# All weights decoded in seven periods, two units at a place, and first expert blocks of 128 and 256 tokens

## The chip, the cores and the metric

The kernel runs on one NeuronCore of a Trainium2 chip. Its engines have queues of their own, each worked off in order: TensorE (PE, with its weight loads as PEld), VectorE (DVE), ScalarE (ACT), GpSimd (POOL), and SyncE (SP), which issues all transfers. The metric is the device time of one execution in microseconds (us), the median of several runs.

## The reference

Attention over 8 batches of 8 heads, 576 tokens and head dimension 64, in which each query keeps its 32 best scores; then a gated layer without activation over the 4608 rows of 512 values that the heads form.

```python
scores = scale * np.matmul(q, k.transpose(0, 1, 3, 2))
kth = np.partition(scores, -top_k, axis=-1)[..., -top_k:-top_k + 1]
scores = np.where(scores >= kth, scores, -1000000000.0)
attn = np.exp(scores - np.max(scores, axis=-1, keepdims=True))
attn = attn / (np.sum(attn, axis=-1, keepdims=True) + 1e-09)
x = np.matmul(attn, v)          # heads of a token side by side
...
a = x @ w1                      # 512 x 1024
b = x @ w2                      # 512 x 1024
h = a * b @ w3                  # 1024 x 1024
return h @ w_out                # 1024 x 512
```

All is float32. The kernel multiplies `w3` and `w_out` once, so that the layer has three products of weights: `w1`, `w2` and the folded `wf`.

## The kernel before, in words

**Slots and periods.** The attention is cut into 144 slots, 18 for each batch: a slot is one pair of heads and 128 queries (for the last 64 queries of a batch, two pairs of heads). The main loop runs over periods p = -1 to 146. In period p TensorE makes the scores of slot p + 1 (`st`), VectorE finds the 32 best of each row of slot p (`fold` into three parts, then MAX8 and MATCH_REPLACE8 by turns: the finder), ScalarE and GpSimd mask slot p - 1 and take its exponentials (`pab`), and TensorE transposes slot p - 2 (`tp`), multiplies it with the values (`ro`) and spreads its sums, after which VectorE normalises it (`rec`) and ScalarE and GpSimd split it into a high and a low part of the type fp32r (`x`).

**The experts.** Twelve slots give 384 tokens of all 512 values, a block. `moe_steps` is a generator of 288 matmuls for a block: for each of 8 parts of the 1024 hidden values twice 12 (`ab`, with weights `wh` and `wl`, the high and low parts), then for each of 4 parts of the output 24 (`eo`, with `wf`). The main loop calls `fill` three times a period, after the masks, after the first exponentials and after the values, and each call takes 8 of them: 24 a period, 288 in the twelve periods in which the next block is collected. The last block is worked off after the loop. Beside its matmuls a block needs, for each of the 8 parts, a copy and a rounding on ScalarE, a product on VectorE (`asb`) and a subtraction on GpSimd (`g`).

**Decoding the weights.** The weights come as 64-bit numbers whose float32 value has to be put together from their halves. There are 80 units of 128 x 256: 16 of `w_out`, then eight times 4 of `w3` and 2 of `w1`, then 16 of `w2`. A unit is a generator whose steps are taken one by one. Step 1: two activations on ScalarE, the first into half of a PSUM tile `t` (two units share a tile, lines 105 to 111), the second inside `z`, the tile that was fetched. Step 2: two operations on VectorE. Step 3: one addition on GpSimd. Step 4: nothing. Step 5: for `w1` and `w2` the high part on ScalarE, for `w3` two products with `wo` on TensorE (`pf`, 4 instructions in the trace). Step 6: the low part on GpSimd (`wl`), or, after each fourth unit of `w3`, the rounding of the folded product on ScalarE (`wf`); step 7: its rest on VectorE.

`warm` stands at six places of a period: after the fold, after the masks, after the first exponentials, after the finder's second round, after its third, and at the end. Before, from period 0 on, each of them starts one unit and takes one step of every unit under way, and then fetches, so that four tiles are on order. 80 units at 6 a period take periods 0 to 13. The first block is complete in period 13, and its matmuls begin in period 14.

**What sets the order.** Engines, wrapped in `InOrder`, get their instructions in the order in which the code is written; nothing sorts them. Transfers share SyncE's queue. Tiles `z` and the experts' `g` share eight buffers, `t`, `pf`, `ab` and `eo` share three PSUM tiles.

Of the kernel before, what the change touches and what calls it, by code (L numbers as in the profile page):

```python
# [19 lines left out]
NHP = H // 2  # L20
# [17 lines left out]
BLOCK = NS * NB // S  # L38
# [4 lines left out]
WAITING = 4  # L43
SHARE = 8, 8, 8
# [23 lines left out]
def attn_moe(ctx: ExitStack, tc: tile.TileContext, q, k, v, w1, w2, w3, w_out, out, flag, general):  # L68
# [354 lines left out]
    n_blocks = n_slots // BLOCK  # L423
    column, places = {}, []
    for n in range(n_blocks):
        mine = sorted({group_of[i] for i in range(n * BLOCK, (n + 1) * BLOCK)}, key=lambda g: groups[g])
        lo, pieces = 0, []
        for g in mine:
            b, t = groups[g]
            column[g], at_, w_ = lo, b * S + t * 128, width(t)  # L430
            if pieces and pieces[-1][0] + pieces[-1][2] == at_:
                pieces[-1][2] += w_
            else:
                pieces.append([at_, lo, w_])
            lo += w_
        assert lo == NB
        places.append([(lambda es, o=o, w_=w_: out[es, o : o + w_], slice(lo, lo + w_)) for o, lo, w_ in pieces])
# [9 lines left out]
    def fill(n):  # L447
        evict()
        while queue and n:
            if next(queue[0], "end") == "end":  # L450
                queue.pop(0)
            else:
                n -= 1

    def begin():
        while starting:
            n = starting.pop(0)
            queue.append(moe_steps([xs[n, hp] for hp in range(NHP)], NB, places[n], put_off.append))
# [22 lines left out]
    def warm():  # L481
        if p < 0:
            return
        if fetched:
            z, step = fetched.pop(0)
            going.append(step(z))
        going[:] = [unit for unit in going if next(unit, "end") != "end"]
        prefetch(WAITING)

    renew_q(0)  # L490
    for hp in range(NHP):
        kts[0, hp] = load_k(0, hp)
        if hp == 0:
            prefetch(WAITING)
    for hp in range(NHP):
        vts[0, hp] = load_v(0, hp)
    renew_q(1)
    for p in range(-1, n_slots + 3):
        i, j, m = p + 1, p - 1, p - 2
        finder = top32_steps(ss[p], p) if 0 <= p < n_slots else iter(())  # L500
# [14 lines left out]
        fill(SHARE[0])  # L515
# [8 lines left out]
        fill(SHARE[1])  # L524
# [21 lines left out]
        fill(SHARE[2])  # L546
        for _ in finder:
            pass
        if 0 <= m < n_slots:
            n = m // BLOCK  # L550
# [8 lines left out]
            if (m + 1) % BLOCK == 0:  # L559
                starting.append(n)  # L560
        warm()
    begin()
    while queue:
        fill(6)
# [63 lines left out]
```

## Time and profile before

| | |
|---|---|
| median of 3 runs | 1333.83 us (1333.48 to 1335.4) |
| the profiled execution's own time | 1335.09 us |
| its span | 1333.3 us |
| busy: PE, DVE | 1244.6 us (93%), 1194.2 us (90%) |
| busy: ACT, POOL | 977.0 us (73%), 750.6 us (56%) |
| mean granted TensorE clock | 0.977 |

Durations below come from the one profiled execution. Its span lies 1.8 us under its own time, and its own time 1.26 us over the median of the runs. Busy shares are means over the whole span: the first 210 us, in which weights are decoded, the steady state after 306 us and the last 63 us, in which one block is left, have different limits, so they are read apart.

### The profile page before, as it was taken

What the parts mean: (1) busy time and instruction counts of PE and PEld (TensorE: products, weight loads), DVE (VectorE), ACT (ScalarE), POOL (GpSimd) and SP (SyncE); (2) the same over time, 40 slices, a digit from 0 to 9 for tenths busy, and PEclk for the clock granted to TensorE, in tenths of its full rate; (3) what the DMA queues carried; (4) which work ended last, traced back from release to release, by engine and by line L of the source; (5) the groups of instructions that cost most, each with busy time, mean ns of one, the idle gap of its engine ahead of it and who ended that gap; (6) DMA issues with size and microseconds to landing.
All of it is one profiled execution on the core that took longest, in us unless ns stands there. A gap on an engine that the chain in (4) does not pass through costs nothing.

```text
span 1333.3 us, 29001 instructions
## 1 busy us (share of the span) xinstructions
PE 1244.6 (93%) x10001; PEld 1060.5 (80%) x10001; DVE 1194.2 (90%) x4012; ACT 977.0 (73%) x2185; POOL 750.6 (56%) x1097
## 2 busy tenths in 40 slices
PE   3677758999999999999999999999999999999996
PEld 1334436888888888888888888888888888888996
DVE  7988899999999999999999999999999999999610
ACT  5766777777777877778877777778777778778621
POOL 4666687655655655655645546645546556555510
PEclk9899978999999999999999999999999999999998
DMA  7233331200021001100120012100210012000000
GB/s 246 83 108 117 106 97 35 74 22 21 29 73 32 9 27 62 53 27 15 39 86 17 9 34 78 31 33 13 65 57 9 15 47 80 22 21 1 14 13 27
DMA packets 35890, 64.89 MB, mean 49 GB/s; under 512 B 6036, under 2 KB 12180, under 8 KB 35732
## 3 DMA queue, kind: packets, MB, share of 16 engines
q1 hardware_dynamic: 35732, 62.93, 14.7%
q8 instruction: 81, 1.33, 0.4%
q14 instruction: 77, 0.63, 0.2%
HBM read 53.48 MB, written 9.44 MB: 47 GB/s over the span
## 4 chain that ended last, share of the span: by engine, by line
PE 86%; DVE 6%; POOL 3%; issue 2%; ACT 2%; DMA 0%; POOLq 0%; SPq 0%
PE ab L57 32%; PE ro L57 16%; PE eo L57 16%; PE st L57 12%; PE tp L57 9%; DVE w L57 2%; DVE z L57 2%; PE pf L57 2%; POOL pab L57 1%; POOL z L57 1%; POOL wl L57 1%; ACT s L57 1%; DVE top L57 0%; ACT pab L57 0%; DVE wf L57 0%
## 5 line engine op out<-in xcount | busy, mean ns | idle before, releaser
L57 POOL TENSOR_TENSOR pab<-s,pab 128x576 f32<-128x576 f32 x288 | 403.7, 1423 | 218.3 <-PE ab L57 130.9
L57 DVE MAX8 top<-w 128x8 f32<-128x192 f32 (+1 forms) x1152 | 467.3, 447 | 0.0
L57 PE MATMUL ab<-x,wh 128*128 128x384 f32 x1536 | 402.6, 343 | 0.0
L57 DVE MATCH_REPLACE8 w<-top,w 128x192 f32<-128x192 f32 x864 | 289.4, 342 | 0.0
L57 ACT COPY pts<-tp 128x1024 f32<-128x1024 f32 x144 | 146.3, 1016 | 185.4 <-PE tp L57 185.4
L57 PEld LDWEIGHTS ab<-x,wh 128*128 128x128 f32 x1536 | 275.1, 189 | 0.0
L57 PE MATMUL ab<-x,wl 128*128 128x384 f32 x768 | 269.7, 351 | 0.0
L57 ACT ACTIVATE pab<-pab,edge 128x576 f32<-128x576 f32 x288 | 227.9, 791 | 0.7 <-POOL pab L57 0.7
L57 PE MATMUL eo<-g,wf 128*128 128x384 f32 x1152 | 225.6, 345 | 0.0
L57 PE MATMUL st<-kt,qt 64*128 64x288 f32 (+1 forms) x1280 | 188.7, 443 | 36.2 <-ACT pts L57 25.3
L57 ACT ACTIVATE pab<-s,edge 128x576 f32<-128x576 f32 x288 | 207.5, 768 | 4.1 <-POOL edge L57 3.9
L57 PEld LDWEIGHTS eo<-g,wf 128*128 128x128 f32 x1152 | 198.5, 188 | 7.5 <-issue 5.7
L57 ACT COPY s<-st 128x576 f32<-128x576 f32 x288 | 186.1, 647 | 17.7 <-PE st L57 17.7
L57 DVE TENSOR_TENSOR w<-s 128x384 f32<-128x384 f32 x288 | 186.7, 689 | 7.3 <-ACT s L57 7.3
L57 PEld LDWEIGHTS st<-kt,qt 64*128 64x128 f32 (+1 forms) x1280 | 100.6, 183 | 98.7 <-issue 41.6
L57 DVE TENSOR_TENSOR w<-w,s 128x384 f32<-128x384 f32 x288 | 165.8, 576 | 4.9
L57 PE MATMUL tp<-ident,pab 128*128 128x128 f32 x1152 | 151.3, 275 | 10.0 <-ACT s L57 9.9
L57 PE MATMUL ro<-pts,vt 128*64 128x128 f32 (+1 forms) x2560 | 157.2, 267 | 0.0
L57 PEld LDWEIGHTS ab<-x,wl 128*128 128x128 f32 x768 | 144.3, 188 | 13.6 <-issue 12.5
L57 PEld LDWEIGHTS tp<-ident,pab 128*128 128x128 f32 x1152 | 135.8, 142 | 21.2 <-POOL wo L57 10.7
L57 PEld LDWEIGHTS ro<-pts,vt 128*64 128x64 f32 x2560 | 137.8, 140 | 0.0
L57 POOL TENSOR_TENSOR g<-asb,g 128x384 fp32r<-128x384 f32 x96 | 97.0, 1010 | 69.6 <-ACT g L57 69.6
(49 smaller groups left out, 1246.7 us busy)
## 6 DMA issues: line engine op xcount, KB each, us to landing
z<-in_w SPq DMA_DIRECT2D x64, 256.0 KB, 2.7
vt<-in_v SPq DMA_DIRECT2D x32, 352.0 KB, 3.6
qt<-in_q SPq DMA_DIRECT2D x40, 256.0 KB, 2.7
kt<-in_k SPq DMA_DIRECT2D x32, 320.0 KB, 3.0
out_t<-osb SPq DMA_DIRECT2D x32, 192.0 KB, 1.9
z<-in_wo SPq DMA_DIRECT2D x16, 256.0 KB, 4.2
out_t<-osb SPq DMA_DIRECT2D x16, 160.0 KB, 1.8
out_t<-osb SPq DMA_DIRECT2D x16, 32.0 KB, 1.6
```

Source lines behind the costliest of these rows:

```text
L57: ins = fn(*args, **kw)
```

## The change

Three things change.

- `UNITS = 2`: each call of `warm` starts a unit and takes a step of all units, and does so twice. `warm` runs in period -1 too. So 12 units are started in a period, 80 in periods -1 to 5. Three tiles are on order instead of four.
- Keys and values of batch 0 are loaded one pair of heads at a time, keys in periods -1 to 2 and values in periods 0 to 3, where all were loaded ahead of the loop. The second tile of queries is loaded in period 0.
- `CUTS`: the first block is 4 slots (128 tokens), the second 8 (256 tokens), then eleven of 12 (384 tokens). A block's share for each call of `fill` follows from the periods in which the next block is collected: 12 matmuls for the first block (8 periods), 8 for all others. The first block's matmuls begin in period 6, the second's in period 14, the third's in period 26.

```diff
--- before.py
+++ after.py
@@ -35,13 +35,13 @@
 
 
 NS = len(slots_of(0))
-BLOCK = NS * NB // S
+CUTS = [0, 4] + list(range(NS * NB // S, B * NS + 1, NS * NB // S))
 NEG = -3.0e38
 STEEP = 2.0**80
 SCALE = 0.125
 S_BUFS = 3
-WAITING = 4
-SHARE = 8, 8, 8
+WAITING = 3
+UNITS = 2
 
 
 class InOrder:
@@ -420,10 +420,11 @@
         if not groups or groups[-1] != (b, t):
             groups.append((b, t))
         group_of.append(len(groups) - 1)
-    n_blocks = n_slots // BLOCK
-    column, places = {}, []
+    n_blocks = len(CUTS) - 1
+    block_of = [n for n in range(n_blocks) for _ in range(CUTS[n], CUTS[n + 1])]
+    column, places, widths = {}, [], []
     for n in range(n_blocks):
-        mine = sorted({group_of[i] for i in range(n * BLOCK, (n + 1) * BLOCK)}, key=lambda g: groups[g])
+        mine = sorted({group_of[i] for i in range(CUTS[n], CUTS[n + 1])}, key=lambda g: groups[g])
         lo, pieces = 0, []
         for g in mine:
             b, t = groups[g]
@@ -433,7 +434,7 @@
             else:
                 pieces.append([at_, lo, w_])
             lo += w_
-        assert lo == NB
+        widths.append(lo)
         places.append([(lambda es, o=o, w_=w_: out[es, o : o + w_], slice(lo, lo + w_)) for o, lo, w_ in pieces])
     last_use = {(b, hp): i for i, (b, hps, t) in enumerate(slots) for hp in hps}
 
@@ -444,10 +445,11 @@
         while put_off:
             put_off.pop(0)()
 
-    def fill(n):
+    def fill():
         evict()
+        n = queue[0][1] if queue else 0
         while queue and n:
-            if next(queue[0], "end") == "end":
+            if next(queue[0][0], "end") == "end":
                 queue.pop(0)
             else:
                 n -= 1
@@ -455,7 +457,9 @@
     def begin():
         while starting:
             n = starting.pop(0)
-            queue.append(moe_steps([xs[n, hp] for hp in range(NHP)], NB, places[n], put_off.append))
+            fills = 3 * (CUTS[n + 2] - CUTS[n + 1]) if n + 1 < n_blocks else 36
+            steps = moe_steps([xs[n, hp] for hp in range(NHP)], widths[n], places[n], put_off.append)
+            queue.append((steps, -(-3 * (2 * NCC * NFC + NFC * NEC) // fills)))
 
     def of(table, b):
         return {hp: table[b, hp] for hp in range(NHP) if (b, hp) in table}
@@ -479,24 +483,24 @@
             fetched.append((fetch(src), step))
 
     def warm():
-        if p < 0:
-            return
-        if fetched:
-            z, step = fetched.pop(0)
-            going.append(step(z))
-        going[:] = [unit for unit in going if next(unit, "end") != "end"]
-        prefetch(WAITING)
+        for _ in range(UNITS):
+            if fetched:
+                z, step = fetched.pop(0)
+                going.append(step(z))
+            going[:] = [unit for unit in going if next(unit, "end") != "end"]
+            prefetch(WAITING)
 
     renew_q(0)
-    for hp in range(NHP):
-        kts[0, hp] = load_k(0, hp)
-        if hp == 0:
-            prefetch(WAITING)
-    for hp in range(NHP):
-        vts[0, hp] = load_v(0, hp)
-    renew_q(1)
+    kts[0, 0] = load_k(0, 0)
+    prefetch(WAITING)
     for p in range(-1, n_slots + 3):
         i, j, m = p + 1, p - 1, p - 2
+        if i + 1 < NHP:
+            kts[0, i + 1] = load_k(0, i + 1)
+        if 0 <= p < NHP:
+            vts[0, p] = load_v(0, p)
+        if p == 0:
+            renew_q(1)
         finder = top32_steps(ss[p], p) if 0 <= p < n_slots else iter(())
         if 0 <= m < n_slots:
             invert(pabs[m][1])
@@ -512,7 +516,7 @@
             for a in range(2):
                 mask(ss[j], edges[j], pabs[j][0], a, folded if a == 0 else None)
         warm()
-        fill(SHARE[0])
+        fill()
         begin()
         next(finder, None)
         if 0 <= m < n_slots:
@@ -521,7 +525,7 @@
         if 0 <= j < n_slots:
             exps(edges[j], *pabs[j], 0)
         warm()
-        fill(SHARE[1])
+        fill()
         next(finder, None)
         warm()
         if i < n_slots:
@@ -543,11 +547,11 @@
             renew(vts, load_v, m)
         next(finder, None)
         warm()
-        fill(SHARE[2])
+        fill()
         for _ in finder:
             pass
         if 0 <= m < n_slots:
-            n = m // BLOCK
+            n = block_of[m]
             for hp in hps:
                 if (n, hp) not in xs:
                     xs[n, hp] = new_x()
@@ -556,12 +560,13 @@
             for part in fresh:
                 split_high(*part)
             del ss[m], pabs[m], edges[m]
-            if (m + 1) % BLOCK == 0:
+            if m + 1 == CUTS[n + 1]:
                 starting.append(n)
         warm()
     begin()
     while queue:
-        fill(6)
+        queue[0] = queue[0][0], 6
+        fill()
     evict()
 
     worst = small.tile([128, B + 1], F32, tag="worst", name="worst", bufs=1)
```

The scheduling of the places shows in each engine's queue. On ScalarE, around the copies of the scores in a period that decodes `w3` and `w1`; `t` and `z` are a unit's two activations, `s` the scores, `pab` the second exponential, `rec` the spread sums, `x` the high part of the normalised slot. Before:

```order
L57 ACTIVATE t_740<-z_660 128x256
L57 ACTIVATE z_660<-z_660 128x256
L57 ACTIVATE t_740<-z_674 128x256
L57 ACTIVATE z_674<-z_674 128x256
L57 COPY s_764<-st_758 128x2x288
L57 ACTIVATE pab_697,sums_698<-pab_697,edge_693 128x576
L57 COPY s_764<-st_761 128x2x288
L57 COPY rec_780<-ro_726 128x128
L57 ACTIVATE t_791<-z_691 128x256
L57 ACTIVATE z_691<-z_691 128x256
L57 CAST x_798<-rec_780 128x128
L57 ACTIVATE t_791<-z_711 128x256
```

The same stretch now:

```order
L57 ACTIVATE t_614<-z_594 128x256
L57 ACTIVATE z_594<-z_594 128x256
L57 COPY s_635<-st_629 128x2x288
L57 ACTIVATE pab_539,sums_540<-pab_539,edge_536 128x576
L57 COPY s_635<-st_632 128x2x288
L57 COPY rec_653<-ro_579 128x128
L57 ACTIVATE t_666<-z_603 128x256
L57 ACTIVATE z_603<-z_603 128x256
L57 ACTIVATE t_666<-z_617 128x256
L57 ACTIVATE z_617<-z_617 128x256
L57 CAST x_682<-rec_653 128x128
L57 ACTIVATE t_690<-z_627 128x256
```

Both units of a shared `t` (`t_666`) now stand together behind the copies; before, one of them (`t_791`) stood there, and the other behind the cast.

On VectorE, the end of the same period; `z` are a unit's two operations, MAX on `w` the last round of the finder, `rec` the normalising. Before:

```order
L57 TENSOR_SCALAR z_674<-t_740 128x256
L57 SCALAR_TENSOR_TENSOR z_674<-t_740,z_674 128x256
L57 MAX top2_97<-w_678 128x8 x2
L57 TENSOR_TENSOR rec_780<-ro_726,rec_780 128x128
L57 TENSOR_SCALAR z_691<-t_791 128x256
L57 SCALAR_TENSOR_TENSOR z_691<-t_791,z_691 128x256
L57 RECIPROCAL sums_698<-sums_698 128x2
```

Now:

```order
L57 TENSOR_SCALAR z_594<-t_614 128x256
L57 SCALAR_TENSOR_TENSOR z_594<-t_614,z_594 128x256
L57 TENSOR_SCALAR z_603<-t_666 128x256
L57 SCALAR_TENSOR_TENSOR z_603<-t_666,z_603 128x256
L57 MAX top2_97<-w_511 128x8 x2
L57 TENSOR_TENSOR rec_653<-ro_579,rec_653 128x128
L57 TENSOR_SCALAR z_617<-t_666 128x256
L57 SCALAR_TENSOR_TENSOR z_617<-t_666,z_617 128x256
L57 TENSOR_SCALAR z_627<-t_690 128x256
L57 SCALAR_TENSOR_TENSOR z_627<-t_690,z_627 128x256
L57 RECIPROCAL sums_540<-sums_540 128x2
```

The first unit that ScalarE starts behind its copies (`z_603`) is decoded ahead of the finder's last round; before, the unit that stands there (`z_691`) was decoded behind it and behind the normalising.

On TensorE, after the last product of decoded weights; `st` are scores, `tp` and `ro` belong to a finished slot. Before, no block is ready yet:

```order
L57 MATMUL tp<-ident,pab 128x128 x8
L57 MATMUL ro<-ident,pab 128x128
L57 MATMUL st<-kt,qt 128x288 x4
L57 MATMUL ro<-ident,sums 64x128 x2
L57 MATMUL ro<-pts,vt 64x128 x8
L57 MATMUL ro<-pr,vt 64x128 x2
```

Now the first block's matmuls of 128 tokens stand between, twelve at a place, three times a period (the last four of one place, then the next):

```order
L57 MATMUL ab<-x,wl_103 128x128
L57 MATMUL ab<-x,wh_98 128x128 x2
L57 MATMUL ab<-x,wl_103 128x128
L57 MATMUL tp<-ident,pab 128x128 x8
L57 MATMUL ro<-ident,pab 128x128
L57 MATMUL ab<-x,wh_99 128x128 x2
L57 MATMUL ab<-x,wl_983 128x128
L57 MATMUL ab<-x,wh_99 128x128 x2
L57 MATMUL ab<-x,wl_983 128x128
```

The transposes, the scores and the values, which stood next to each other, are parted by them.

## Rows read from the trace of the kernel before

**Rows 1.** Busy time of each engine by stretches: start and end of the stretch, its length, then busy us and number of instructions of PE, PEld, DVE, ACT and POOL, the granted TensorE clock, the share of the DMA engines and GB/s. The stretches end at the folds of periods 0, 14 and 26.

```profile
0.00:7.33 7.33, 2.29 (x8) 1.27 (x8) 0.00 (x1) 2.60 (x4) 1.03 (x9) 1.00 0.74 257
7.33:209.61 202.28, 132.76 (x650) 72.89 (x651) 178.27 (x529) 142.33 (x354) 136.30 (x188) 0.88 0.36 115
209.61:306.28 96.67, 94.47 (x884) 82.62 (x883) 93.37 (x321) 75.21 (x166) 59.20 (x87) 0.98 0.15 47
306.28:1258.08 951.80, 951.80 (x8073) 841.61 (x8072) 916.54 (x3150) 741.25 (x1628) 544.24 (x803) 1.00 0.11 35
```

**Rows 2.** Timeline of ScalarE in the steady state, the copies of two transposed slots: start, length, engine, line, operation, tiles, shape, and in brackets the idle time before it with what ended it.

```profile
1202.53 1.02 ACT L57 COPY pts<-tp 128x1024 f32<-128x1024 f32 x1 [1.30 <-PE tp L57]
...
1210.57 1.02 ACT L57 COPY pts<-tp 128x1024 f32<-128x1024 f32 x1 [1.31 <-PE tp L57]
```

**Rows 3.** The chain that ended last, its last two long pieces: start, length, what.

```profile
1270.39 33.92 PE ab L57 x192
1304.31 16.96 PE eo L57 x96
```

**Rows 4.** Timeline of VectorE in periods that decode `w3` and `w1`, folds and what ends its waits, and the fold of period 14.

```profile
89.08 1.54 DVE L57 TENSOR_TENSOR w<-s 128x384 f32<-128x384 f32 x2
...
105.50 1.54 DVE L57 TENSOR_TENSOR w<-s 128x384 f32<-128x384 f32 x2
...
108.32 0.41 DVE L57 TENSOR_SCALAR z<-t 128x256 int32<-128x256 int32 x1
...
109.10 0.68 DVE L57 TENSOR_TENSOR wf<-pf,wf 128x512 fp32r<-128x512 f32 x1
...
110.49 0.61 DVE L57 MAX8 top<-w 128x8 f32<-128x192 f32 x2
...
116.64 1.41 DVE L57 MAX8 top<-w 128x8 f32<-128x576 f32 x2
118.74 0.29 DVE L57 TENSOR_TENSOR rec<-ro,rec 128x128 f32<-128x128 f32 x1 [0.68 <-ACT rec L57]
119.39 0.42 DVE L57 TENSOR_SCALAR z<-t 128x256 int32<-128x256 int32 x1 [0.36 <-ACT z L57]
...
209.61 1.58 DVE L57 TENSOR_TENSOR w<-s 128x384 f32<-128x384 f32 x2
```

**Rows 5.** Timeline of GpSimd in the same period: the two masks together, and the addition of a unit.

```profile
109.57 2.78 POOL L57 TENSOR_TENSOR pab<-s,pab 128x576 f32<-128x576 f32 x2 [1.59 <-ACT pab L57]
...
113.00 0.72 POOL L57 TENSOR_TENSOR z<-z 128x256 int32<-128x256 int32 x1
```

**Rows 6.** Timeline of TensorE: products of decoded weights (four instructions are one unit) in three periods, and the eight transposes of a slot in the steady state.

```profile
103.55 3.70 PE L57 MATMUL pf<-wo,z 128*128 128x512 f32 x8
...
113.78 1.98 PE L57 MATMUL pf<-wo,z 128*128 128x512 f32 x4 [2.53 <-POOL z L57]
...
128.54 3.20 PE L57 MATMUL pf<-wo,z 128*128 128x512 f32 x4 [2.54 <-POOL z L57]
...
161.36 1.98 PE L57 MATMUL pf<-wo,z 128*128 128x512 f32 x4 [2.54 <-POOL z L57]
...
1209.44 1.03 PE L57 MATMUL tp<-ident,pab 128*128 128x128 f32 x8
```

**Rows 7.** Timeline of ScalarE in one decoding period, from the masks on.

```profile
108.73 1.43 ACT L57 ACTIVATE pab<-s,edge 128x576 f32<-128x576 f32 x2
...
111.28 0.99 ACT L57 COPY pts<-tp 128x1024 f32<-128x1024 f32 x1
...
116.49 0.64 ACT L57 COPY s<-st 128x576 f32<-128x576 f32 x1 [0.93 <-PE st L57]
117.03 0.78 ACT L57 ACTIVATE pab<-pab,edge 128x576 f32<-128x576 f32 x1
...
117.80 0.63 ACT L57 COPY s<-st 128x576 f32<-128x576 f32 x1
118.44 0.27 ACT L57 COPY rec<-ro 128x128 f32<-128x128 f32 x1
118.60 0.41 ACT L57 ACTIVATE t<-z 128x256 f32<-128x256 f32 x1
...
120.31 0.41 ACT L57 ACTIVATE t<-z 128x256 f32<-128x256 f32 x1 [0.76 <-DVE z L57]
```

**Rows 8.** The same view as in rows 1, of the whole period that begins with the fold at 105.50 and of two of the bursts in rows 6.

```profile
105.50:120.27 14.77, 11.18 (x59) 5.81 (x58) 13.32 (x42) 10.99 (x27) 10.17 (x14) 1.00 0.35 108
128.54:131.67 3.13, 3.13 (x4) 0.88 (x4) 2.96 (x11) 0.83 (x3) 2.69 (x4) 0.60 0.67 226
161.36:163.27 1.91, 1.91 (x4) 0.68 (x4) 1.78 (x8) 0.82 (x3) 1.91 (x3) 1.00 0.61 145
```

**Rows 9.** Timeline of ScalarE at the very start: its first copy of scores, and the second of two units that share a tile.

```profile
5.70 0.64 ACT L57 COPY s<-st 128x576 f32<-128x576 f32 x1 [3.69 <-PE st L57]
...
10.24 0.40 ACT L57 ACTIVATE t<-z 128x256 f32<-128x256 f32 x1 [2.29 <-DVE z L57]
```

**Rows 10.** Groups of instructions by form: line, engine, operation, tiles, shapes, number, then busy us and mean ns of one, then idle us before.

```profile
L57 PE MATMUL tp<-ident,pab 128*128 128x128 f32 x1152 | 151.3, 275 | 10.0 <-ACT s L57 9.9
...
L57 DVE TENSOR_TENSOR asb<-ab,asb 128x384 f32<-128x384 f32 x96 | 52.6, 548 | 32.5 <-PE ab L57 32.5
...
L57 DVE TENSOR_TENSOR rec<-ro,rec 128x128 f32<-128x128 f32 x144 | 42.0, 291 | 56.6 <-ACT rec L57 50.6
```

## The prediction, before the changed kernel was run

> **What bounds the kernel now.** I read the stages first [rows 1]. From 306.28 to 1258.08 us TensorE is busy all the time and VectorE 916.54 of 951.80 us. That is the steady state: one period takes 8.04 us, from one copy of the transposed weights to the next [rows 2], and VectorE works 7.74 us of it (96.3%). The last block runs alone at the end: 192 and 96 matmuls of 384 columns in 33.92 and 16.96 us, 0.177 us each [rows 3]. Neither stretch changes: the last eleven blocks have the same 384 tokens and the same turns. So the change is decided before 306.28 us: in the 14 periods in which weights are decoded (7.33 to 209.61 us) and in the 12 periods of the first block (96.67 us). In the 202.28 us of decoding VectorE is busy 178.27. All that VectorE does there has to be done in the changed kernel too; what a rearrangement can win is the 24 us that it waits, plus what the first 7.33 us leave idle, and it can lose any amount.
>
> Next I asked what VectorE waits for in one decoding period, 105.50 to 120.26 us. It is a ring through all engines. VectorE folds the scores, decodes a unit, splits a folded weight and decodes another until 110.49 [rows 4]; GpSimd masks for 2.78 us from 109.57 and only then adds the unit of which TensorE's product is next in line, at 113.00 [rows 5]; that product starts at 113.78 [rows 6]; behind it in TensorE's queue stand the scores, behind these ScalarE's two copies, an exponential and the copy of the sums at 118.44 [rows 7]. For these VectorE waits 0.68 us at 118.74, and for the next decode, queued behind them on ScalarE, 0.36 us more [rows 4]. Where TensorE runs at its lower level the same four instructions take 3.20 instead of 1.98 us [rows 6], with a mean granted clock of 0.60 against 1.00 [rows 8], and the period is 16.4 instead of 14.77 us: the folds at 89.08 and 105.50 lie that far apart [rows 4].
>
> **The change, part by part.** *Two units at a place.* Both units of a place share one PSUM tile, and ScalarE's activations of the second wait until VectorE has finished the first: before, 2.29 us at 10.24 and 0.76 us at 120.31 [rows 9, 7]. With one unit at a place the two engines are a whole place apart, and the finder's rounds lie between. With two, VectorE decodes the first unit in the same place in which ScalarE starts it, so at every place the order is ScalarE first unit, VectorE first unit, ScalarE second unit, and whatever ScalarE had to do earlier in the period now stands in front of VectorE.
>
> I lay one such period out by hand, with a unit at 0.75 us on ScalarE and 0.8 on VectorE (119.39 to 120.19) [rows 7, 4], counted from the fold. VectorE: fold 2.8, unit left over 0.8, weight split 0.6, first unit 0.8: 5.0. ScalarE: second unit 0.75, two masks 1.4, first unit of place 2 0.75: 7.9. VectorE decodes it: 8.7. ScalarE: second unit 0.75, pts and pr 1.1, exponential 0.8, first unit of place 3 0.75: 12.1. VectorE: 12.9. ScalarE: second unit; then the rounding of the fold product, which waits for TensorE. GpSimd can mask only from 6.5 (ScalarE's half of the masking stands behind its second unit), ends at 9.3, subtracts one low part and adds the first unit by 10.8 (0.7 each) [rows 5]; TensorE then needs about 1.7 us for each of two units, as pf x8 takes 3.70 with its tail [rows 6], and is done at 14.3. ScalarE: rounding 0.55, high part 0.35, first unit of place 4 0.75: 16.1; VectorE: 16.9. ScalarE: second unit 0.75, copy, exponential, copy, sums (2.1 together, from 116.49 to 118.60), first unit of place 5 0.75: 20.6. VectorE: unit 0.8, MAX8 over 576 1.35, normalising 0.3: 23.0. ScalarE: x 0.3, first unit of place 6 0.75: 24.1; VectorE 0.8: **25.0 us** with the passing of semaphores. VectorE's own work in it is 18.7 us: 13.32 in the period read above [rows 8], six more units of 0.8 and one more split of 0.6. So 6.3 us of waiting in one period that takes the place of two, which waited 1.5 and 3.1 us (14.77 and 16.4, less 13.32).
>
> The low level of TensorE's clock comes on top. The products now stand in groups of four units behind the values, then idle for 2 us and more until GpSimd has added again, then two units in front of the transposes and two in front of the scores. In this trace a burst after 2.54 us of idling ran once at the full and once at the lower level [rows 6, 8]. Nothing lost is one bound; the other is two units at half the clock, 3.4 us more. I take 1.2 us, the difference of the two rows: 26.2 us a period.
> The Trainium skill (TensorE: Matmul & The Clock Gate, "HAM oscillation — how this bites in real kernels") says that bursts parted by idle gaps each start at the lower clock, again and again. By that rule the last rival below would be the likeliest; the two bursts above agree with it one time in two.
>
> *The sum for decoding.* Period -1 now decodes 12 units with nothing between them: each pair costs ScalarE two units and VectorE one, 2.4 us, six pairs 14.4 us from about 5 us on (ScalarE's first work stood at 5.70 [rows 9]), and the copies of the first scores: the first fold near 20 us instead of 7.33. Period 0 has no masks and no values and is bound by VectorE: 18.7 less 0.5 for the sums and their product, 18.2. Period 1 has masks but no values: 24 (the ring without pts, pr and x, 1.4 us, and most of the clock's price). Periods 2 and 3: 26.2 each. Period 4: 26.4, with two more high parts of w2 in the ring. Period 5 has eight units of w2, which cost GpSimd two operations each, but no products: 21. Sum 162 us at the fold of period 6.
>
> *Eight periods with 128-token matmuls.* Each has 36 matmuls of 128 columns instead of none. The trace has no such matmul. Lower bound: in proportion to the columns, 0.059 us. Upper bound: a whole 384-column one, 0.177, or twice a transpose, 0.216. The nearest row is the transpose, which has the same 128 x 128 weight and 128 columns: eight in 1.03 us with a tail of 0.275, 0.108 each [rows 6, 10]. I take that: TensorE 36 x 0.108 + 3.8 = 7.7 us (3.8 is 8.04 less 24 x 0.177). VectorE: 7.74 less 0.37 (two thirds of an asb product of 0.548) plus 1.5 products of about 0.29, a PSUM product of 128 columns [rows 10]: 7.8. With the 0.3 us that the steady state adds: 8.1 us, eight periods 64.8. At the lower bound VectorE still makes it 8.1; at the two upper ones TensorE makes it 10.2 and 11.6.
> So the fold of period 14 comes at 226.8 us, where it came at 209.61 [rows 4]: **17.2 us later**. The seven periods are dear because attention is no cheaper alone than the steady 8 us.
>
> *The 256-token block.* 24 matmuls a period of at most 0.177 us: never dearer than before. If they are cheaper VectorE is the limit: 7.74 less 0.37 plus two thirds of 0.42 is 7.65 us, with some waiting 7.85, against 96.67 / 12 = 8.06 now. Twelve periods: 2.5 us won (0 to 4).
>
> *The rest.* Three tiles fetched ahead instead of four, eight buffers as before: a unit's transfer is issued when the unit five before it is done, over a place ahead of its use, some 4 us in these long periods. Keys and values come a period at a time, each one period or more before its use. I cost both at nothing; if a transfer does come late, ScalarE stands still and the period grows by as much.
>
> The sum: 17.2 - 2.5 = 14.7 us on the profiled execution's 1335.09, 1349.8; the median of the runs is 1.26 lower, so **1348.5 us**.
>
> **The rivals.** *Faster: the engines slip past each other.* If ScalarE runs ahead (its own work is 17 us of such a period: 10.99 [rows 8], six units, two high parts and a rounding more), the hand-laid ring is too strict, and periods 1 to 4 take 20 us each (VectorE's 18.7 and 1.3 of waiting) instead of 102.8 together: 23 us less, and period 5 4 us less: 1321.5. It decides once a decoding period is under about 22.5 us. For it: in the trace VectorE waits only 1.5 us in a good period. Against it: that is with one unit a place, and the queues are in order, so ScalarE cannot start a unit before the copies in front of it. *No change:* decoding periods of 22.5 us, 14 us less: 1334.5. *Much slower: narrow matmuls are not cheaper.* At 0.177 the eight periods take 10.2 us each, 17 us more: 1365.5; at 0.216 28 us more: 1376.5. For it: no row shows a matmul of this kind under 384 columns. Against it: transposes of 128 columns run at 0.108, and TensorE has 0.3 us a period to spare there.
> *Slower by the clock:* every group of products starts at the lower level, 2.2 us more in each of periods 1 to 4: 1357.5.
>
> **How the numbers follow.** The forecast gets 0.48, with a range of its own from 1339 to 1358 (5 us for the clock that stays up, and 4 to 9 us for the stretches that were only estimated); the clock that is always low 0.08, since it rose within a burst in this trace; the faster rival 0.18, no change 0.08, the narrow matmuls 0.18. A measurement of this kernel can tell 0.2%, 2.7 us. Slower by more than that: forecast, clock and narrow matmuls, 0.74; faster 0.18; within 0.08. The range runs from 1327, a third of the way out of the faster rival, to 1368, past the first price of the narrow matmuls.
>
> **What would show it.** Right: folds of periods 2 and 3 that lie 24 to 28 us apart, with VectorE idle 5 us and more before decodes that wait for ScalarE; the first 128-column matmul near 165 us; pitch near 0.11 us; the fold of period 14 near 227 us; the same 8.04 us after it; the same last 51 us. Wrong: decoding periods near 20 us (then faster), periods above 10 us with narrow matmuls (then slower still), or ScalarE waiting for transfers of z, which I cost at nothing.

## The result and the profile after

The changed kernel takes 1344.73 us (median of 4 runs, 1343.74 to 1346.71) against 1334.62 for the kernel before beside it: ratio 1.0074, 95% interval 1.0054 to 1.0095. It is slower, by more than the 0.2% that can be told, as forecast; 1348.5 was 3.8 us too high. The profiled execution took 1343.74 us with a span of 1341.9, the one before 1333.3.

The stages first, in the view of [rows 1]: start and end, length, then busy us and instructions of PE, PEld, DVE, ACT and POOL, granted clock, DMA share, GB/s. The stretches end at the folds of periods 0, 6, 14 and 26.

```profile
0.00:20.05 20.05, 4.58 (x16) 2.46 (x16) 8.89 (x23) 10.04 (x25) 8.15 (x19) 1.00 0.86 287
20.05:164.86 144.81, 89.48 (x319) 44.28 (x319) 108.39 (x300) 89.64 (x236) 90.55 (x131) 0.84 0.44 130
164.86:227.57 62.71, 60.30 (x582) 53.41 (x583) 60.65 (x218) 48.88 (x114) 41.95 (x59) 0.95 0.05 12
227.57:317.21 89.64, 84.42 (x933) 72.74 (x932) 89.15 (x323) 73.54 (x168) 64.09 (x84) 1.00 0.16 50
317.21:1266.70 949.49, 948.67 (x8048) 837.81 (x8048) 915.56 (x3150) 740.53 (x1627) 552.20 (x805) 1.00 0.12 35
```

The decoding periods fill the first two lines: VectorE works 108.39 of 144.81 us, where it worked 178.27 of 202.28 us. In the third and fourth line it is busy 97% and 99% of the time. Period 26 begins 317.21 - 306.28 = 10.9 us later than before; of the rest, 1341.9 - 317.21 = 1024.7 us, it took 1027.0 before.

The folds that begin periods 1 to 6, in VectorE's timeline (start, length, what):

```profile
38.51 1.57 DVE L57 TENSOR_TENSOR w<-s 128x384 f32<-128x384 f32 x2
63.54 1.57 DVE L57 TENSOR_TENSOR w<-s 128x384 f32<-128x384 f32 x2
89.32 1.57 DVE L57 TENSOR_TENSOR w<-s 128x384 f32<-128x384 f32 x2
115.86 1.58 DVE L57 TENSOR_TENSOR w<-s 128x384 f32<-128x384 f32 x2
141.97 2.10 DVE L57 TENSOR_TENSOR w<-s 128x384 f32<-128x384 f32 x2
164.86 1.57 DVE L57 TENSOR_TENSOR w<-s 128x384 f32<-128x384 f32 x2
```

Where a period goes is seen in period 2. ScalarE's timeline in it (in brackets the idle time before an instruction, and what ended it):

```profile
68.92 0.40 ACT L57 ACTIVATE t<-z 128x256 f32<-128x256 f32 x1 [3.46 <-DVE z L57]
...
69.58 1.43 ACT L57 ACTIVATE pab<-s,edge 128x576 f32<-128x576 f32 x2
70.91 0.38 ACT L57 ACTIVATE t<-z 128x256 f32<-128x256 f32 x1
71.23 0.41 ACT L57 ACTIVATE z<-z 128x256 int32<-128x256 uint16 x1
72.59 0.41 ACT L57 ACTIVATE t<-z 128x256 f32<-128x256 f32 x1 [0.95 <-DVE z L57]
72.95 0.42 ACT L57 ACTIVATE z<-z 128x256 int32<-128x256 uint16 x1
74.31 1.01 ACT L57 COPY pts<-tp 128x1024 f32<-128x1024 f32 x1 [0.95 <-PE tp L57]
```

And VectorE's in the same place 2:

```profile
71.68 0.42 DVE L57 TENSOR_SCALAR z<-t 128x256 int32<-128x256 int32 x1 [1.09 <-ACT z L57]
72.14 0.42 DVE L57 SCALAR_TENSOR_TENSOR z<-t,z 128x256 int32<-128x256 int32 x1
```

The first unit is activated at 70.91, decoded on VectorE at 71.68, and ended by 72.56; only then, at 72.59, does ScalarE start the second, after 0.95 us of idling. VectorE had waited 1.09 us for ScalarE just before. The engines take turns, pair by pair. VectorE's waits for ScalarE in period 2 sum up to (engine, what it waited for: us in total, times, longest):

```profile
DVE z L57 <- ACT z L57: 6.2, 5, 2.5
```

And over the second stage, in the same view:

```profile
ACT t L57 <- DVE z L57: 46.8, 35, 3.6
DVE z L57 <- ACT z L57: 28.7, 25, 3.2
```

The groups of TensorE's products in periods 2 and 3:

```profile
67.60 5.80 PE L57 MATMUL pf<-wo,z 128*128 128x512 f32 x8 [6.12 <-issue]
74.62 3.70 PE L57 MATMUL pf<-wo,z 128*128 128x512 f32 x8 [0.24 <-POOL z L57]
80.88 7.13 PE L57 MATMUL pf<-wo,z 128*128 128x512 f32 x16
93.38 6.56 PE L57 MATMUL pf<-wo,z 128*128 128x512 f32 x8 [5.37 <-issue]
```

The group behind the long idle time is slow and the later ones are not; the windows of the first two (columns as above) give the clock:

```profile
67.60:73.40 5.80, 5.80 (x10) 2.50 (x11) 3.79 (x13) 3.50 (x8) 3.99 (x6) 0.63 0.18 49
74.62:78.32 3.70, 3.70 (x10) 1.51 (x10) 1.29 (x4) 2.69 (x8) 2.21 (x4) 1.00 0.67 179
```

The first block's matmuls of 128 columns, in TensorE's timeline:

```profile
172.65 0.39 PE L57 MATMUL ab<-x,wh 128*128 128x128 f32 x2
172.87 0.27 PE L57 MATMUL ab<-x,wl 128*128 128x128 f32 x1
172.99 0.39 PE L57 MATMUL ab<-x,wh 128*128 128x128 f32 x2
```

Three start in 0.34 us (172.65 to 172.99): 0.113 each. Over the whole trace the median from one start to the next is 0.112 us at 128 columns, 0.119 at 256 and 0.176 at 384: the matmuls of the second block, with twice the columns, cost hardly more than those of the first. The steady state and the last block are what they were in [rows 2, 3], from ScalarE's timeline and the chain of waits:

```profile
1203.75 1.02 ACT L57 COPY pts<-tp 128x1024 f32<-128x1024 f32 x1 [1.31 <-PE tp L57]
1211.79 1.02 ACT L57 COPY pts<-tp 128x1024 f32<-128x1024 f32 x1 [1.31 <-PE tp L57]
```

```profile
1279.64 33.92 PE ab L57 x192
1313.56 16.96 PE eo L57 x96
```

### The profile page after: what moved, and what is told of

The parts are those of the page before. It is cut to its first block, busy times and chain, and to the rows that moved or that the text cites. A ratio compares the mean times of both kernels' runs of the same rounds, so it can differ in the third digit from the quotient of the medians.

```text
span 1341.9 us, 29628 instructions
## 1 busy us (share of the span) xinstructions
PE 1251.4 (93%) x10289; PEld 1073.4 (80%) x10289; DVE 1188.7 (89%) x4020; ACT 978.7 (73%) x2205; POOL 767.4 (57%) x1105
## 4 chain that ended last, share of the span: by engine, by line
PE 83%; DVE 8%; ACT 3%; issue 3%; POOL 2%; DMA 0%; SPq 0%; DVEq 0%; POOLq 0%; ACTq 0%
PE ab L57 31%; PE ro L57 15%; PE eo L57 15%; PE st L57 11%; PE tp L57 9%; DVE w L57 3%; DVE top L57 2%; DVE z L57 2%; PE pf L57 2%; POOL wl L57 1%; ACT z L57 1%; ACT pab L57 1%; POOL z L57 1%; ACT t L57 1%; ACT s L57 0%
## 5 line engine op out<-in xcount | busy, mean ns | idle before, releaser
L57 PE MATMUL ab<-x,wh 128*128 128x384 f32 (+2 forms) x1664 | 418.4, 335 | 2.7 <-POOL x L57 2.7
L57 PEld LDWEIGHTS ab<-x,wh 128*128 128x128 f32 x1664 | 292.4, 189 | 4.7 <-POOL x L57 2.9
L57 PE MATMUL ab<-x,wl 128*128 128x384 f32 (+2 forms) x832 | 282.9, 340 | 0.0
L57 ACT ACTIVATE pab<-pab,edge 128x576 f32<-128x576 f32 x288 | 227.5, 790 | 10.3 <-POOL pab L57 10.3
L57 PE MATMUL eo<-g,wf 128*128 128x384 f32 (+2 forms) x1248 | 232.1, 336 | 0.0
L57 PE MATMUL st<-kt,qt 64*128 64x288 f32 (+1 forms) x1280 | 184.8, 435 | 30.9 <-ACT pts L57 17.4
L57 PEld LDWEIGHTS eo<-g,wf 128*128 128x128 f32 x1248 | 205.1, 188 | 8.1 <-issue 6.3
L57 DVE TENSOR_TENSOR w<-s 128x384 f32<-128x384 f32 x288 | 178.8, 661 | 0.0
L57 PEld LDWEIGHTS ab<-x,wl 128*128 128x128 f32 x832 | 156.9, 189 | 12.5 <-issue 11.6
L57 PEld LDWEIGHTS st<-kt,qt 64*128 64x128 f32 (+1 forms) x1280 | 97.3, 178 | 85.7 <-issue 32.1
L57 POOL TENSOR_TENSOR g<-asb,g 128x384 fp32r<-128x384 f32 (+2 forms) x104 | 98.5, 947 | 69.6 <-ACT g L57 69.4
```

The source lines that it names most:

```text
L57: ins = fn(*args, **kw)
```

## The experiments

The theory at the outset: the loss lies in the decoding stage, because the two units of a place share a tile `t` and so tie ScalarE to VectorE; the narrow blocks give a part back. The rivals: narrow matmuls that are not cheaper, the clock, and the queue order of TensorE. The kernel before was run again beside each set of experiments, with medians from 1334.62 to 1336.34 us, so a difference between kernels of two sets is uncertain by up to 1.7 us; ratios are to the kernel before of the same set.

**The early decoding without the narrow blocks.**

```diff
-CUTS = [0, 4] + list(range(NS * NB // S, B * NS + 1, NS * NB // S))
+CUTS = list(range(0, B * NS + 1, NS * NB // S))
```

> The changed kernel with blocks of 384 tokens from the first on; decoding in seven periods stays. Theory (the decoding periods cost the time, the narrow blocks give some back): the fold of period 6 stays at 165 us; periods 6 to 13 have no expert matmuls and take VectorE's own 7.35 us, fold of period 14 at 224; the first block's twelve periods take 94 us, fold of period 26 at 318; the rest 1027 us. Time some 3 us above the changed kernel's, 11 to 13 above the kernel before. Rival (the narrow matmuls, with a weight load for every 128 or 256 columns, cost the time): with them gone the time falls to the kernel before's, within 3 us.

Measured: 1352.27 us, ratio 1.0133 (1.0116 to 1.0150), span 1350.0: 7.5 us above the changed kernel, where some 3 were expected. Its stages between the folds of periods 6, 14 and 26:

```profile
165.31:227.52 62.21, 43.37 (x323) 29.78 (x323) 58.95 (x209) 45.12 (x95) 36.47 (x50) 0.76 0.03 10
227.52:322.98 95.46, 93.94 (x888) 82.25 (x889) 92.22 (x322) 75.35 (x167) 62.55 (x86) 1.00 0.15 48
```

The eight periods cost 62.21 us without any expert matmul and 62.71 with 36 narrow ones in each: these hide behind VectorE, and that rival falls. The twelve periods behind them cost 95.46 instead of 89.64. So the early decoding alone costs 1350.0 - 1333.3 = 16.7 us of the span, and the narrow blocks give back 8.1 of them.

**Two tiles for a pair.** Four units in a row now take the first half of `t0`, the first of `t1`, the second of `t0` and the second of `t1`, so that neighbours stand in different tiles.

```diff
-            both = ps_m.tile([128, 512], F32, tag="mm", name="t")
-            bank.extend((both[:, 256:], both[:, :256]))
+            t0, t1 = (ps_m.tile([128, 512], F32, tag="mm", name="t") for _ in range(2))
+            bank.extend((t1[:, 256:], t0[:, 256:], t1[:, :256], t0[:, :256]))
```

> The changed kernel, but the two units of a place write into halves of two PSUM tiles instead of one, so ScalarE's second unit no longer waits for VectorE's first. Theory (the ring ScalarE - VectorE - ScalarE at each place): the first fold comes at 15 to 16 us instead of 20, periods 1 to 4 take 1.5 to 2 us less each (near 24), period 5 stays (GpSimd), fold of period 6 near 153; time 12 us under the changed kernel's, 1331 to 1334. Rival (TensorE's products and GpSimd's additions in front of the scores set the period, or TensorE's lower clock): periods 1 to 4 stay at 25 to 26.5, and only the first fold moves; 4 us less.

Measured: 1335.82 us, ratio 1.0002 (0.9992 to 1.0011), 8.9 us under the changed kernel, where 12 were expected. The first fold comes at 17.39 instead of 20.05, that of period 6 at 154.63 instead of 164.86. The waits of its decoding stage:

```profile
ACT t L57 <- DVE z L57: 19.2, 16, 3.0
DVE z L57 <- ACT z L57: 16.9, 17, 3.7
...
ACT pts L57 <- PE tp L57: 10.8, 3, 4.5
```

The two engines wait 36 us for each other instead of 75.5, so the tile was the tie behind about half of these waits. Only 10.2 us of the 39 come off by the fold of period 6. A new wait shows: ScalarE's copy of the transposes. In period 2 it waits 4.5 us for them, and the period does not get shorter (26.17 us, 25.78 with one tile). In TensorE's queue these stand behind a group of products at the low clock:

```profile
61.70 6.62 PE L57 MATMUL pf<-wo,z 128*128 128x512 f32 x8 [5.58 <-issue]
68.16 1.04 PE L57 MATMUL tp<-ident,pab 128*128 128x128 f32 x8
```

**The same edit on the kernel before.**

> The kernel before with halves of two tiles. Theory: there one unit stands at a place, so only the wait at the end of a period goes (0.76 us in the trace), in nine periods or so: 3 to 7 us less than the kernel before. Rival: no change, since the period there is set by the masks, the products and the scores, in 0.3%.

Measured: 1333.54 us, ratio 0.9983 (0.9974 to 0.9993): 2.4 us, less than expected. With one unit at a place the tile costs little. (Its ten runs spread from 1329.41 to 1334.29, and the profiled one was the lowest, so its span of 1327.6 shows a larger gain than the median does.)

**Two tiles without the narrow blocks.**

> Halves of two tiles and blocks of 384 tokens from the first on, decoding in seven periods. If the two effects are independent: 3 us above the changed kernel with two tiles, some 9 us under the one with wide blocks alone. If the narrow blocks are worth more once decoding ends earlier (or less), the two differences do not add up.

Measured: 1340.30 us, ratio 1.0040 (1.0026 to 1.0054). The narrow blocks are worth 4.5 us here and 7.5 with one tile (1352.27 - 1344.73); the tile is worth 8.9 us with them and 12.0 without. The two don't simply add, and why not was not followed up.

**The transposes ahead of the products**, on two tiles; the same lines were moved in the changed kernel as it is.

```diff
+        if 0 <= m < n_slots:
+            tp, ro = turn(pabs[m][0])
         warm()
         fill()
         begin()
         next(finder, None)
         if 0 <= m < n_slots:
-            tp, ro = turn(pabs[m][0])
             pts, pr = take_turned(tp, ro)
```

> The kernel with two tiles for t, and the nine transposes of the finished slot put ahead of place 2 in TensorE's queue. Theory (once ScalarE no longer waits for VectorE within a pair, the copy of the transposes is held by the products of place 2 that stand in front of them, 4.50 and 3.25 us of waiting for tp in the periods from 57.03 and 83.20 us): these waits go, periods 2 to 4 become about 3 us shorter each, so 1335.8 - 9 = 1327 us. Rival (the products themselves are late, and the copies of fold products and scores that follow wait for them as long as before): the wait moves to those copies and the time stays at 1334 to 1337 us.

> The changed kernel (one tile for a pair) with the same move of the nine transposes and nothing else. Theory (in the changed kernel ScalarE and VectorE hold each other in pairs, and TensorE's order hardly matters: ScalarE waited only 0.95 us for tp): 0 to 3 us less than the changed kernel, 1342 to 1345 us. Rival (TensorE's order bound it there too): 9 us less, 1336 us.

Measured: 1330.79 us on two tiles, ratio 0.9968 (0.9956 to 0.9981), 5.0 us less than two tiles alone; on one tile 1344.53, ratio 1.0074 (1.0057 to 1.0091), no change. So TensorE's order costs something only once the tie is gone, and half of what I expected. No wait of ScalarE for `tp` is left in the decoding stage, but its waits for the fold product (`pf`) grow from 5.6 to 13.3 us, which is what the rival expected of the whole gain, and a period still takes 23.6 us with 19.07 of VectorE's work.

**Keeping TensorE's clock up.** To the kernel with the transposes first, 40 more transposes of the identity into columns of `ro` that nothing reads:

```diff
             tp, ro = turn(pabs[m][0])
+            for _ in range(40 if waiting else 0):
+                pe.transpose(ro[:, 384:], ident, ident)
```

> As the first kernel of this set, with 40 more transposes of the identity into unused columns behind the nine transposes, in periods that decode: work for TensorE while it would stand idle before the products of place 2. They add nothing to the result. If the low granted clock of the products (eight in 6.62 and 5.37 us against 3.60 at the full clock) holds the periods up: 1 to 3 us less in each of periods 2 to 4 than without them, 3 to 9 us in all. If it doesn't, the same time within 2 us. If the transposes are still running when the first unit is ready, some us more.

Measured: 1331.01 us, ratio 0.9968 (0.9958 to 0.9979), the same as without. Period 3, first without and then with them:

```profile
80.76:104.36 23.60, 19.75 (x76) 9.45 (x75) 19.07 (x53) 16.01 (x43) 15.15 (x23) 0.93 0.53 150
```

```profile
81.64:105.25 23.61, 22.21 (x116) 13.22 (x115) 19.18 (x54) 16.10 (x43) 15.13 (x23) 1.00 0.52 147
```

The granted clock rises from 0.93 to 1.00, and the period keeps its length to 0.01 us. The products of period 2 without and with them show why:

```profile
61.83 9.06 PE L57 MATMUL pf<-wo,z 128*128 128x512 f32 x16 [4.61 <-issue]
```

```profile
62.72 3.67 PE L57 MATMUL pf<-wo,z 128*128 128x512 f32 x8 [0.23 <-issue]
68.09 3.70 PE L57 MATMUL pf<-wo,z 128*128 128x512 f32 x8 [1.69 <-POOL z L57]
```

At the full clock the first eight end 1.7 us before GpSimd has added the next unit; at the low clock TensorE is only busy until then. Both ways the sixteenth ends 13.7 us behind the fold. (In the profiled execution periods 1 and 5 grew by 1.5 and 0.9 us, and its span is 2.1 us longer; the medians lie 0.2 apart.) The clock is no cause in periods 2 to 4, once the transposes stand ahead of the products.

**One unit at each of twelve places**, first with two tiles, then with the one tile of the changed kernel: `UNITS = 1`, and six more calls of `warm()` between the six, as here:

```diff
         fresh.clear()
+        warm()
         if 0 <= j < n_slots:
             pabs[j] = new_weights()
...
         next(finder, None)
+        warm()
         if 0 <= m < n_slots:
             tp, ro = turn(pabs[m][0])
```

> The kernel with two tiles for t, with one unit at each of twelve places in a period instead of two at each of six; as many units in as many periods. Theory (what makes a decoding period of 12 units dear is that units stand in pairs, so that ScalarE's copies for the slot and VectorE's rounds of the finder queue behind two units each): periods 1 to 4 fall from 25 us to 21 to 23, 8 to 14 us less than 1335.8, so 1322 to 1328 us. Rival (the ring through GpSimd and TensorE binds however the units stand): 1334 to 1338 us.

> The changed kernel with its one tile for two units kept, and one unit at each of twelve places. Theory (the tile costs time only because its two units stand at one place: ScalarE needs the tile back before VectorE has got to the first unit): with a place between them the tile costs little, 1330 to 1334 us. Rival (a half place is too short, and the tile ties the engines together as before): within 3 us of the changed kernel, 1341 to 1345 us. Between them, say 1337 us: both count.

Measured: 1328.87 us with two tiles, ratio 0.9955 (0.9938 to 0.9972), and 1340.40 with one, ratio 1.0032 (1.0020 to 1.0044). Spreading is worth 6.9 and 4.3 us, the tile 8.9 us in pairs and 11.5 spread. By the ratios, each to the kernel before beside it, it is 6.3 and 5.6 us for spreading and 9.6 and 10.3 for the tile, so the tile costs about as much either way. My theory that it costs only where both units stand at one place falls; the rival fits, by which half a place between them is too short. The waits of the decoding stage with one tile, spread, have hardly changed:

```profile
ACT t L57 <- DVE z L57: 42.0, 35, 3.3
...
DVE z L57 <- ACT z L57: 26.5, 25, 3.6
```

**All three together, and two kernels beside them:** two tiles, twelve places and transposes first; the kernel before with two tiles and transposes first; and all three with `WAITING = 4`.

> Both edits that helped at once: two tiles for t, one unit at each of twelve places, and the nine transposes put ahead of the products of place 2 (now its first half) in TensorE's queue. In the spread kernel ScalarE still waits 11.5 us for the transposes (five times, 3.6 us the longest). If these waits bind there as they did with pairs (4 to 5 us for the move): 1323 to 1326 us, below both kernels. If the spread already took what they cost: 1328 to 1330 us.

> The kernel before (one unit at a place, first block of 384 tokens) with two tiles for t and the nine transposes ahead of place 2: the two repairs that fit both kernels. It tells whether decoding in seven periods is worth anything once it isn't hindered. If the kernel before waits for the transposes too: 3 to 6 us less than its 1333.5 with two tiles, so 1328 to 1330, and the early decoding, spread and repaired (1325.2), is worth 3 to 5 us. If the transposes did not hold it: 1332 to 1334, and the early decoding is worth 7 to 9 us.

> The spread kernel with the transposes first (1325.2) and four tiles on order instead of three, as before the change. The prediction costed the shorter order at nothing. In that kernel ScalarE waits for a transfer of z 1.00, 0.35 and 0.20 us in three decoding periods. If these waits are on the path, 1 to 1.5 us less: 1324. If nothing hangs on them: 1325.2 within 1 us.

Measured: all three 1325.24 us, ratio 0.9923 (0.9909 to 0.9936), the fastest of this study; the kernel before with its two repairs 1334.43, ratio 0.9989 (0.9981 to 0.9998); four tiles on order 1325.87, ratio 0.9932 (0.9919 to 0.9945), no change. Of the fastest, its decoding stage and the eight periods behind it:

```profile
16.91:145.26 128.35, 84.91 (x318) 42.36 (x318) 106.28 (x301) 88.32 (x234) 94.85 (x131) 0.90 0.51 153
145.26:208.61 63.35, 61.52 (x585) 54.43 (x585) 60.77 (x217) 48.61 (x114) 41.34 (x59) 0.94 0.04 12
```

The decoding stage is 16.5 us shorter than the changed kernel's for the same work; 22 us in it are still VectorE's waiting. So decoding in seven periods together with the narrow blocks is worth 9 us against the kernel before with the two repairs that fit it (1334.43 - 1325.24); as the change made it, the tile, the pairs and TensorE's order cost more than that, 19.5 us (1344.73 - 1325.24). How much of the 9 us the narrow blocks give was not tried in this kernel; with two tiles in pairs they were worth 4.5 us, and early decoding without them lost (1340.30 against 1333.54). Side by side, folds in us:

| kernel | median | first fold | fold of period 6 | fold of period 14 |
|---|---|---|---|---|
| changed | 1344.73 | 20.05 | 164.86 | 227.57 |
| changed, twelve places | 1340.40 | 19.66 | 160.23 | 224.30 |
| two tiles | 1335.82 | 17.39 | 154.63 | 218.53 |
| two tiles, transposes first | 1330.79 | 17.20 | 150.49 | 213.91 |
| two tiles, twelve places | 1328.87 | 16.97 | 148.67 | 212.23 |
| all three | 1325.24 | 16.91 | 145.26 | 208.61 |

## Why the prediction was right

The direction and the place were right: the ring of a decoding period is longer than VectorE's work in it. The trace follows the ring as it was laid out, and the experiments confirm the tile as one part of it. Step by step, in us of the profiled executions:

| step | forecast | measured |
|---|---|---|
| first fold | 20 | 20.05 |
| periods 0 and 1 | 18.2, 24 | 18.46, 25.03 |
| periods 2, 3, 4 | 26.2, 26.2, 26.4 | 25.78, 26.54, 26.11 |
| period 5 | 21 | 22.89 |
| eight periods of 128 tokens | 64.8 | 62.71 |
| fold of period 14 | 226.8 | 227.57 |
| twelve periods of 256 tokens | 94.2 | 89.64 |
| the rest against before | 0 | -2.3 |

*The ring.* The hand-laid period holds unit by unit. Counted from the fold of period 2 (63.54), VectorE ended the first unit of place 2 at 9.0 (laid out 8.7), that of place 3 was ready on ScalarE at 13.4 (12.1), that of place 4 at 16.6 (16.1), that of place 5 at 21.1 (20.6), and the period ended at 25.8 (25.0 and 1.2 for the clock). The share of the tile in it is measured: 10.2 us at the fold of period 6, of which 2.7 lie ahead of the first fold. That is not the whole ring. In periods 1 to 4 VectorE waits 27.6 us (103.46 us long, 75.90 of work); two tiles shorten them by 5.0 us, all three repairs by 12.6, and in the fastest kernel VectorE still waits 16.7 us there (90.85 less 74.19). What sets that rest was not tried. The six pairs of the start began 2.48 us apart at first (7.45, 9.93, 12.43), where 2.4 was forecast.

*The clock.* 1.2 us a period was taken for it. In period 2 a group at the low level took 5.80 us instead of 3.70, and the copy of the transposes behind it waited 0.95 us, so the size is plausible there. But with the transposes moved ahead in the changed kernel that wait is gone, and periods 2 to 4 took 25.43, 25.44 and 26.09 us: 1.5 us less in the three, where 3.6 were put down to the clock. The rest of the 3.6 is not shown to be the clock's, so that the sum fits each period is partly luck. Lifting the clock was not tried in the changed kernel itself; with two tiles and the transposes moved it won nothing. The rule named beside this term (the Trainium skill, TensorE: Matmul & The Clock Gate, "HAM oscillation — how this bites in real kernels") agrees with the trace for the first group of periods 2 to 4: behind 5 to 6 us of idling it starts low (5.80, 6.56, 5.25 us). The second group, with less than 1 us of idling before it, runs at 3.60 to 3.70, and in period 1 two groups behind 3.04 and 3.34 us of idling took 3.67 and 3.70 us. The rival that I drew from the rule, every group slow and 2.2 us a period more, did not come: most groups ran at the full clock, and in period 2 the slow one ended at 73.40, 1.2 us before GpSimd's next unit let TensorE go on with the products (74.62).

*Period 5* was 1.9 us too low. GpSimd is busy 19.53 of its 22.89 us, with two operations for each unit of `w2`; the addition to the sums, queued among them, lets VectorE's reciprocal wait 2.78 us. I had named the two operations and not costed their queue.

*The narrow matmuls.* 0.108 was taken from the transposes, 0.113 measured; both upper bounds are out. The eight periods came to 7.84 us, 7.58 of VectorE's work and 0.26 of waiting, where 7.8 and 0.3 were taken. (The block after it was taken as "at most 0.177"; its 256-column matmuls start 0.119 us apart.)

*What was off: the 256-token block and the rest.* For the profiled execution the sum gave 1349.8, and it took 1343.74: 6.1 us too much, 4.5 in the twelve periods and 2.3 behind them, less 0.8 at the fold of period 14. (By the medians it is 3.8, since the profiled execution of before lay above the median of the runs and that of after below.) I took 7.85 us a period, 7.65 of VectorE's work and 0.2 of waiting. Measured are 7.47, with 7.43 of work (89.15 / 12) and next to no waiting, in a stretch in which TensorE is busy 84.42 of 89.64 us. And "rest unchanged" failed: in the third block the periods stay at 7.4 to 7.9 us from the fold at 317.21 on (324.61, 332.47, 340.40), before the 8.04 us come back. Over these twelve periods that makes 1.7 of the 2.3 us; the rest lies later and was not followed.

*Transfers* were costed at nothing, rightly: in the decoding stage ScalarE waits for no transfer of `z`, and four tiles on order won nothing in the fastest kernel.

*The faster rival*, 20 us for each of periods 1 to 4, did not come, not even with its obstacles taken out: in the fastest kernel they take 22.3 to 23.0 us (folds at 33.88, 56.22, 79.17, 101.88, 124.73), the pace that I gave for "no change". That the total is 1325 all the same comes from the other stages: the first fold 3 us earlier and the twelve periods and the third block shorter than in the sum. The sum for "no change" was off besides: four periods of 22.5 us in place of 102.8 are 12.8 us less, not 14, so 1335.7 instead of 1334.5.

## What to carry to other kernels

A tile shared by two neighbouring units of a pipeline is a wait between the engines that fill and empty it: put neighbours into different tiles before they are moved closer together, at one place or half a place apart. In the kernel before, with six units a period, the same tile cost 2.4 us; with twelve, 9 to 12. Where a wait goes, look in each queue for what stands in front of the next one waited for; the move of nine transposes was worth nothing before the tile was split and 5 us after. Work that TensorE does at its lower clock should not be counted as a cost until it is shown that somebody waits for its end.

## What the runs showed that I had not expected

Halves of one PSUM tile with no element in common tie the engines as if they were one place: 46.8 us of ScalarE's waiting over the decoding stage with one tile, 19.2 with two, for the same instructions. Whether the program's bookkeeping or the memory asks for that wait, these runs don't tell.

VectorE's fold takes longer where it meets GpSimd. By form, first of the twelve periods from 227.57 us and then of twelve periods of the same kernel in its steady state (600.00 to 696.50 us), busy us and mean ns:

```profile
L57 DVE TENSOR_TENSOR w<-s 128x384 f32<-128x384 f32 x25 | 13.2, 564 | 0.0
```

```profile
L57 DVE TENSOR_TENSOR w<-s 128x384 f32<-128x384 f32 x24 | 15.6, 688 | 0.0
```

It is the same operation on tiles of the same shape, 0.12 us apart. One fold of each stretch, with GpSimd's subtraction beside it or behind it:

```profile
605.13 1.30 DVE L57 TENSOR_TENSOR w<-s 128x384 f32<-128x384 f32 x2
605.55 0.46 POOL L57 TENSOR_TENSOR x<-rec,x 128x128 fp32r<-128x128 f32 x1 [0.74 <-ACT x L57]
```

```profile
257.86 1.56 POOL L57 TENSOR_TENSOR edge<-top,coef 128x4 f32<-128x4 f32 x1 [0.94 <-DVE top L57]
257.90 1.00 DVE L57 TENSOR_TENSOR w<-s 128x384 f32<-128x384 f32 x2
...
259.53 0.78 POOL L57 TENSOR_TENSOR x<-rec,x 128x128 fp32r<-128x128 f32 x1
```

At 605 us the fold's second operation starts at 605.58, inside the subtraction that ends at 606.01, and ends at 606.43, 0.42 us behind it. At 257.90 no subtraction runs beside the two, and neither is longer than 0.55 us; here it is GpSimd's small operation `edge` that takes 1.56 us, where it takes 0.20 at 604.46. So it is in the whole trace. A fold has four such operations, 576 in all; 151 of them take over 0.6 us, and each of these started while a subtraction or an addition of GpSimd was running and ended 0.41 to 0.42 us behind its end, while the other 425 take 0.53 to 0.58 us. In the twelve periods 6 of 48 are long, in the steady state 12 of 48, in the six decoding periods 12 of 24, at some 1.1 us each. So VectorE's busy time holds waiting for GpSimd, 6 us of it in the decoding stage. No run moved GpSimd's work to test this.

For the twelve periods this means: of the 4.5 us by which they were overestimated, 2.6 are VectorE's work (7.65 - 7.43 us, twelve times), 2.0 of them in the folds, and 1.9 the waiting that did not come.
